# First bias of two head pairs read back in four pieces, small weights placed ahead of GpSimd's masks, first copies of reciprocals moved to VectorE

## The chip, the core and the metric

The kernel runs on one core of a Trainium2 chip. The metric is the device time of one execution in microseconds. The engines work side by side, each through its own queue in order: TensorE (PE, with its weight loads as PEld), VectorE (DVE), ScalarE (ACT), GpSimd (POOL) and SyncE (SP), which here issues most of the transfers.

## What is computed

An attention layer with a learned bias on relative positions, then a dense layer with a gated norm, then a layer of eight experts with two chosen for each token. Only the first touches the change:

```python
scores = scale * np.matmul(q, k.transpose(0, 1, 3, 2))        # 2 batches, 8 heads, 576 x 576, 64 wide
psi_rel = np.log1p(np.abs(rel)); psi_i = np.log1p(np.maximum(pos[:, None], 1.0))
x = (psi_rel / psi_i)[..., None]
h = np.maximum(x @ w1 + b1, 0.0)                               # 32 hidden units
bias = h @ w2                                                  # one value for query, key and head
scores = scores + bias.transpose(2, 0, 1)[None]
attn = np.exp(scores - scores.max(-1)); attn = attn / (attn.sum(-1) + 1e-9)
out = np.matmul(attn, v)
```

## The kernel before

A hidden unit is on or off depending on where |query - key| lies against a threshold, so the bias is made from masks. One **m** stands for 32 queries; there are 18. `masks(m, ...)` makes eight masks of 128 x 576 (four queries by 32 hidden units on the partitions), each on VectorE, ScalarE or GpSimd by the letters of MASK_ENG0 (m = 0: VectorE and ScalarE in turn), MASK_ENG1 (m = 1 to 6: GpSimd for masks 1 and 6, VectorE for 4, ScalarE for the other five) and MASK_ENG2 (from m = 7: five on GpSimd, three on VectorE). Masks have three buffers (`mk`). `mix(m, gg)`, called twice for an m, multiplies four masks with the small weights `WD` on TensorE (L204; slopes and intercepts, each as two fp16 parts), and VectorE joins them into the bias tile `t` (L209, L210; three buffers). After the second call SyncE writes `t` to a scratch tensor in DRAM, `biasd` (L212), since the bias is made with the queries in another order over the partitions than the scores need.

The small weights: `wab`, `W`, the scaling of `W`, and `WD` with its remainder are seven short operations on GpSimd (L150 to L173), with a power of two as scale that VectorE finds in between (L160 to L167).

Attention then goes over five blocks of 128 queries (`it`), four pairs of heads (`hp`) and two batches (`b`), one step k for each. `bias_in(n)` reads the bias of block it = n // 4 and pair hp = n % 4 back from `biasd` into the tile `bt` (128 x 2 x 576, six buffers); a block needs four m, so `bias_in(0)` and `bias_in(1)` need the writes of m = 0 to 3. `qk` makes scores (L308), adds bias and finds the row's extreme in one VectorE operation (L317), and ScalarE takes the exponential (L324). `tr` transposes the result, and, at the second batch, makes reciprocals of the sums (L343, L344) and spreads them over 64 columns into `rb` (L347, on GpSimd). `av` transposes `rb` (L359), multiplies with v (L368) and scales on VectorE (L372).

The program's order: all masks of m = 0, the products of m = 0 to 5 (twelve calls of `bias_step`, each of which also asks for masks of the next m), then `bias_in(0)` and `bias_in(1)`, then the steps k, each with one further `bias_step`, a `bias_in` at every second step, and from step 4 on the conversion of 64-bit weights, spread over the engines. The order on each engine's queue is not this one: the framework's scheduler simulates the program ahead of time, and whenever an engine is free it hands it the earliest instruction that is ready. `tc.keep_in_program_order(i)` pins an instruction behind the instruction that was written before it for the same engine. `tc.high_priority()` around the small weights puts them first among what is ready.

Of the kernel before, what the change touches and what calls it, by code (L numbers as in the profile page):

```python
# [9 lines left out]
F32 = mybir.dt.float32  # L10
# [6 lines left out]
OP = mybir.AluOpType  # L17
# [3 lines left out]
B, H, S, D = 2, 8, 576, 64  # L21
# [10 lines left out]
EB = 8  # L32
LAG = 2
PRE = 6
XB = 9
WB = 12
XS = (2, 2, 2, 2, 0, 1, 0, 1, 2)
# [27 lines left out]
def build(tc, I, O):  # L65
    nc = tc.nc
    ctx = ExitStack()
    with ctx:
        _build(tc, nc, ctx, I, O)


def _build(tc, nc, ctx, I, O):
# [4 lines left out]
    biasd = dram.tile([NG, 128, S], F32, name="biasd")  # L77
# [8 lines left out]
    V, P_ = nc.vector, nc.gpsimd  # L86
# [3 lines left out]
    def pool(stack, name, **kw):  # L90
        return stack.enter_context(tc.tile_pool(name=name, bufs=1, **{"reuse_waits": "tile", **kw}))

    xap, bp = pool(px, "xap"), pool(px, "bp")
    kvp, btp, ap = pool(pa, "kvp"), pool(pa, "btp"), pool(pa, "ap")
# [6 lines left out]
    def dbank():  # L101
        return psum.tile([128, 2, 512], F32, name="d", bufs=3)
# [27 lines left out]
    thr = bp.tile([128, 2, NQ], F32, name="thr")  # L130
# [45 lines left out]
    def engine(m, u):  # L176
        return (MASK_ENG0 if m == 0 else MASK_ENG1 if m < PRE + 1 else MASK_ENG2)[u]

    MK, TT = {}, {}

    def masks(m, lo, hi):

        if lo == 0:
            MK[m] = bp.tile([128, 8, S], BF, name="mk", bufs=3)
        for u in range(lo, hi):
            q, dst = 8 * m + u, MK[m][:, u]
            w = T[:, 572 - 4 * q:1148 - 4 * q]
            e = engine(m, u)
            if e == "A":
                nc.scalar.activation(dst, w, AF.Sigmoid, bias=thr[:, 1, q:q + 1], scale=STEP)  # L190
            else:
                (V if e == "D" else P_).tensor_scalar(dst, w, thr[:, 0, q:q + 1], None, op0=OP.is_gt)  # L192

    def mix(m, gg):

        if gg == 0:
            TT[m] = bp.tile([128, 2, S], F32, name="t", bufs=3)
        mk, G = MK[m], 2 * m + gg
        sl, ic = dbank(), dbank()
        for a, ps in enumerate((sl, ic)):  # L200
            for half in range(2):
                for n in range(2):
                    for u in range(4):
                        nc.tensor.matmul(ps[32 * u:32 * u + 32, half, 0:288], WD[n][:, 32 * a:32 * a + 32],  # L204
                                         mk[:, 4 * gg + u, half * 288:half * 288 + 288],
                                         start=(n == 0), stop=(n == 1))
        th = TT[m][:, gg].rearrange("p (a b) -> p a b", a=2)
        Lw = L[:, 560 - 16 * G:560 - 16 * G + S].rearrange("p (a b) -> p a b", a=2)
        V.scalar_tensor_tensor(th, Lw, inv[:, G:G + 1], sl[:, :, 0:288], op0=OP.mult, op1=OP.mult)  # L209
        V.scalar_tensor_tensor(th, ic[:, :, 0:288], unscale, th, op0=OP.mult, op1=OP.add)  # L210
        if gg == 1:
            nc.sync.dma_start(biasd[2 * m:2 * m + 2].rearrange("g p j -> p g j"), TT.pop(m))  # L212

    def bias_step(s):

        m, gg = divmod(s, 2)
        if m >= NM:
            return
        if m + 1 < NM:
            masks(m + 1, 4 * gg, 4 * gg + 4)  # L220
        mix(m, gg)

    BT = {}

    def bias_in(n):

        it, hp = divmod(n, 4)
        if it > 4:
            return
        r = 8 if it < 4 else 4  # L230
        src = biasd[8 * it:8 * it + r].rearrange("g (q h) j -> (g q) h j", h=H)[:, 2 * hp:2 * hp + 2]
        t = BT[it, hp] = btp.tile([128, 2, S], F32, name="bt", bufs=6)
        if it < 4:
            nc.sync.dma_start(t, src)
        else:
            for x in range(2):
                nc.sync.dma_start(t[64 * x:64 * x + 64, 0], src[:, x])
# [62 lines left out]
    def qk(it, hp, b):  # L300

        n, k = 2 * hp + b, KV[hp, b]
        if it < 4:
            ss = [dbank() for x in range(2)]
            for a in range(2):
                for x in range(2):
                    h = slice(64 * x, 64 * x + 64)
                    nc.tensor.matmul(ss[x][:, a, 0:288], Q[it][h, n], k[h, a * 288:a * 288 + 288], start=True, stop=True)  # L308
        else:
            ss = [dbank()]  # L310
            for a in range(2):
                nc.tensor.matmul(ss[0][:, a, 0:288], Q[it][:, n], k[:, a * 288:a * 288 + 288], start=True, stop=True)
        es = []
        for x, ps in enumerate(ss):
            e = ap.tile([128, S], F32, name="e", bufs=EB)
            nm = ap.tile([128, 1], F32, name="nm", bufs=6)
            V.tensor_tensor_reduce(out=e.rearrange("p (a b) -> p a b", a=2), in0=ps[:, :, 0:288],  # L317
                                   in1=BT[it, hp][:, x].rearrange("p (a b) -> p a b", a=2),
                                   scale=-0.125, scalar=3.0e38, op0=OP.add, op1=OP.min, accum_out=nm)
            es.append((e, nm))  # L320
        u = unit(it, hp)
        c = b * len(es)
        for x, (e, nm) in enumerate(es):
            nc.scalar.activation(e, e, AF.Exp, bias=nm, scale=-1.0, accum_out=u.sums[:, c + x:c + x + 1])  # L324
        ES[it, hp, b] = [e for e, nm in es]

    def tr(it, hp, b):

        u, es = SU[it, hp], ES.pop((it, hp, b))
        n = len(es)  # L330
        if b == 0:
            u.rest = psum.tile([128, 4, 128], F32, name="rest")
        pt = dbank().rearrange("p x (j i) -> p x j i", j=4)
        for x, e in enumerate(es):
            for jb in range(4):
                nc.tensor.transpose(pt[:, x, jb], e[:, jb * 128:jb * 128 + 128], ident)  # L336
        for x, e in enumerate(es):
            nc.tensor.transpose(u.rest[:, n * b + x], e[:, S - 128:S], ident)
        nc.scalar.activation(u.et[:, n * b:n * b + n, 0:4], pt[:, 0:n], AF.Copy)  # L339
        if b == 1:  # L340
            nc.scalar.activation(u.et[:, 0:2 * n, 4], u.rest[:, 0:2 * n], AF.Copy)
            u.rs = ap.tile([128, 4], F32, name="rs", bufs=3)
            V.tensor_scalar(u.rs[:, 0:2 * n], u.sums[:, 0:2 * n], 1e-9, None, op0=OP.add)  # L343
            V.reciprocal(u.rs[:, 0:2 * n], u.rs[:, 0:2 * n])  # L344
            if n == 2:
                u.rb = ap.tile([128, 4, 64], F32, name="rb", bufs=2)
                P_.tensor_copy(u.rb, u.rs[:, :, None].to_broadcast([128, 4, 64]))  # L347

    def av(it, hp):

# [21 lines left out]
        V.tensor_tensor(out=dst, in0=dst, in1=o[:, 1, :, 0:n], op=OP.mult)  # L372

    masks(0, 0, 8)
    for s in range(2 * PRE):
        bias_step(s)
    tc.keep_in_program_order(nc.scalar.preload_act_table_set("natural_log_exp_and_others"))
    bias_in(0)
    bias_in(1)
    chunks = list(range(16))  # L380
    raws, conv = [], []
    for k in range(len(A) + LAG + 8):
        if k % 2 == 0 and k < len(A):
            bias_in(k // 2 + 2)
        if k % 8 == 6 and k // 8 + 1 < 5:
            load_q(k // 8 + 1)
        if LAG <= k < len(A) + LAG:
            tr(*A[k - LAG])
        if LAG <= k - 1 < len(A) + LAG and A[k - 1 - LAG][2] == 1:
            av(*A[k - 1 - LAG][:2])  # L390
        if k < len(A):
            qk(*A[k])
        bias_step(2 * PRE + k)
        if k == CONV[0] - 3:
            raws = [words(chunks.pop(0)) for c in range(RB64)]
        if k in CONV:
            n = CONV.index(k)
            conv.append([5] + (conv_out(n, raws.pop(0)) if n < 8 else conv_in(*divmod(n - 8, 2), raws.pop(0))))
        for fs in conv:
            if len(fs) > 1:  # L400
                fs.pop(1)()
                fs[0] -= 1
                if fs[0] == 0 and chunks:
                    raws.append(words(chunks.pop(0)))
# [81 lines left out]
    def stage2(t, mid):  # L486
        lt = LT.pop(t)
        po = (abank, tbank)[t % 2 if AB else 0]()
        for f in range(8):
            for n, (wx, ww) in enumerate(PASSES):  # L490
                nc.tensor.matmul(po, lt[wx][:, f], WO[f][ww], start=(f == 0 and n == 0), stop=(f == 7 and n == 2))
            if f == FM:
                mid()
        x1 = X1[t] = mp.tile([128, 512], F32, name="x1", bufs=XB)
        nc.scalar.activation(x1, po, AF.Copy, scale=ST.pop(t)[:, 7:8])
# [304 lines left out]
    for e in range(E):  # L800
        W2 = [wload(w2s(e, f), ep, W2B, held=True) for f in range(4)] if e else []
        xt, w1 = XG.pop(e), W1.pop(e)
        for f in range(8):
            ph = psum.tile([128, 512], F32, name="phe", tag="h", bufs=3)
            for k in range(4):
                for n, (ww_, wx) in enumerate(PAS):
# [4 lines left out]
                                   op0=OP.max, op1=OP.subtract)  # L811
# [125 lines left out]
```

## Time and profile before

| | |
|---|---|
| time, median of 3 | 634.76 us (633.47 to 637.0) |
| the profiled execution's own time | 632.79 us |
| its span, first to last instruction | 630.9 us |
| TensorE busy | 581.1 us, 92% |
| VectorE busy | 392.2 us, 62% |
| ScalarE busy | 339.7 us, 54% |
| GpSimd busy | 229.3 us, 36% |
| mean granted clock of TensorE | 0.984 of 2.4 GHz |
| largest transfers: weights of the experts | 64 loads of 512 KB |
| writes of the bias | 18 of 576 KB |
| reads of the bias | 16 of 576 KB |

The shares are averages over stages with different limits: what a change to one stage is worth is read from that stage. All times inside the run are counted from the start of the span.

### The profile page before, as it was taken

The numbers are of one execution on the slowest core, as the hardware profiler recorded it, in microseconds if no ns is written. First come the engines' busy times: TensorE is split into PE (matmuls) and PEld (weight loads), VectorE is DVE, ScalarE is ACT, GpSimd is POOL, SyncE is SP. The second block draws the span as 40 slices with busy tenths as digits, with TensorE's granted clock in tenths as the row PEclk, the third lists the DMA queues.
The fourth block names the chain that finished last, engine by engine and source line by source line (L and its number), as shares of the span: only waits on it lengthen the run. The fifth ranks groups of instructions, "written<-read, shape, count | busy, mean of one in ns | idle before, by whom it ended". The sixth has DMA issues, their size and how long they took to land. (4 is left out here: it accounts for less than half of the span.)

```text
span 630.9 us, 12806 instructions
## 1 busy us (share of the span) xinstructions
PE 581.1 (92%) x5068; PEld 475.8 (75%) x5068; DVE 392.2 (62%) x913; ACT 339.7 (54%) x657; POOL 229.3 (36%) x173
## 2 busy tenths in 40 slices
PE   0879999999999999999999989999999999999990
PEld 0547766767677776888888788989898989898980
DVE  4978889998755636645347968674746464554400
ACT  6935756565678767534337436454545455544410
POOL 4999998990022148000003003221222222222111
PEclk9989999999999999999999989999999999999997
DMA  8675535627532135200405055756566565735212
GB/s 315 261 258 185 213 126 208 240 91 272 204 114 68 52 98 173 85 18 34 151 18 162 23 201 154 206 188 172 196 164 214 146 232 128 240 52 194 35 19 30
DMA packets 36247, 93.64 MB, mean 148 GB/s; under 512 B 3856, under 2 KB 5392, under 8 KB 36176
## 3 DMA queue, kind: packets, MB, share of 16 engines
q1 hardware_dynamic: 28784, 76.23, 33.7%
q0 software_dynamic: 5808, 13.37, 10.5%
q10 hardware_dynamic: 1584, 3.11, 1.4%
q8 instruction: 42, 0.69, 0.5%
q14 instruction: 29, 0.24, 0.1%
HBM read 69.76 MB, written 22.94 MB: 147 GB/s over the span
## 5 line engine op out<-in xcount | busy, mean ns | idle before, releaser
L192 POOL TENSOR_SCALAR mk<-T,thr 128x576 bf16<-128x576 f16 x67 | 119.7, 1805 | 10.7 <-PE d L204 7.2
L807 PE MATMUL phe<-xgt,wp 128*128 128x320 f32 x768 | 117.3, 312 | 2.3 <-ACT xgt L409 2.3
L807 PEld LDWEIGHTS phe<-xgt,wp 128*128 128x128 f32 x768 | 114.6, 190 | 3.0 <-ACT xgt L409 2.5
L641 POOL DMA_INDIRECT out<-y,si x24 | 39.0, 1623 | 149.6 <-ACT y L797 73.1
L790 PE MATMUL poe<-wp,hT 128*128 128x512 f32 x384 | 91.0, 393 | 0.0
L790 PEld LDWEIGHTS poe<-wp,hT 128*128 128x128 f32 x384 | 71.0, 188 | 14.2
L324 ACT ACTIVATE e<-e,nm 128x576 f32<-128x576 f32 x72 | 55.3, 770 | 43.6 <-DVE nm L317 43.6
L204 PE MATMUL d<-mk,wd 128*32 128x288 bf16 x1152 | 49.2, 298 | 26.5 <-POOL wd L171 14.4
L204 PEld LDWEIGHTS <-wd 128*32 128x32 f16 x1152 | 29.6, 98 | 47.7 <-issue 24.0
L810 DVE SCALAR_TENSOR_TENSOR hT<-phe,hT 128x320 fp32r<-128x320 f32 x64 | 31.3, 489 | 51.6 <-ACT hT L809 51.3
L317 DVE CUSTOM_DVE_ANT_0 e<-d,bt 128x576 f32<-128x576 f32 x72 | 51.9, 753 | 12.0 <-PE d L308 7.2
L410 DVE TENSOR_TENSOR wp<-w2raw,wp 128x1024 fp32r<-128x1024 f32 x32 | 39.1, 1225 | 19.2 <-ACT wp L409 17.4
L809 ACT ACTIVATE hT<-phe 128x320 fp32r<-128x320 f32 x64 | 28.0, 438 | 42.6 <-PE phe L807 42.6
L308 PE MATMUL d<-kv,q 64*128 64x288 f32 x256 | 48.0, 438 | 0.3 <-DVE t L210 0.3
L368 PE MATMUL av<-et,kv 128*64 128x128 f32 (+1 forms) x800 | 47.3, 266 | 0.0
L669 POOL DMA_INDIRECT xg<-x1d,gi x21 | 21.7, 1033 | 63.3 <-DVE si L631 47.3
L368 PEld LDWEIGHTS av<-et,kv 128*64 128x64 f32 x800 | 41.2, 137 | 4.4 <-issue 3.9
L336 PE MATMUL d<-ident,e 128*128 128x128 f32 x288 | 40.7, 283 | 2.1 <-ACT et L339 1.9
L339 ACT ACTIVATE et<-d 128x1024 f32<-128x1024 f32 (+1 forms) x40 | 37.2, 930 | 9.1 <-PE d L336 9.1
L452 PE MATMUL ps<-mk,xs 128*128 128x512 f32 x162 | 39.7, 397 | 2.1 <-DVE so L461 1.2
L336 PEld LDWEIGHTS d<-ident,e 128*128 128x128 f32 x288 | 31.9, 143 | 12.8 <-DVE nm L317 6.9
L409 ACT ACTIVATE wp<-w2raw 128x1024 fp32r<-128x1024 f32 x32 | 34.0, 1061 | 13.1 <-DMA w2raw<-moe_w 6.4
(193 smaller groups left out, 958.6 us busy)
## 6 DMA issues: line engine op xcount, KB each, us to landing
wraw<-moe_w SPq DMA_DIRECT2D x32, 512.0 KB, 7.5
w2raw<-moe_w SPq DMA_DIRECT2D x32, 512.0 KB, 6.1
biasd<-t SPq DMA_DIRECT2D x18, 576.0 KB, 3.7
bt<-biasd SPq DMA_DIRECT2D x16, 576.0 KB, 5.9
kv<-kv SPq DMA_DIRECT2D x8, 608.0 KB, 10.0
raw<-w_out SPq DMA_DIRECT2D x8, 512.0 KB, 4.7
raw<-w_in SPq DMA_DIRECT2D x8, 512.0 KB, 3.5
q<-q SPq DMA_DIRECT2D x5, 512.0 KB, 5.0
```

The lines of the kernel that those rows point to most:

```text
L192: (V if e == "D" else P_).tensor_scalar(dst, w, thr[:, 0, q:q + 1], None, op0=OP.is_gt)
L204: nc.tensor.matmul(ps[32 * u:32 * u + 32, half, 0:288], WD[n][:, 32 * a:32 * a + 32], mk[:, 4 * gg + u, half * 288:half * 288 + 288], star ...
L308: nc.tensor.matmul(ss[x][:, a, 0:288], Q[it][h, n], k[h, a * 288:a * 288 + 288], start=True, stop=True)
L317: V.tensor_tensor_reduce(out=e.rearrange("p (a b) -> p a b", a=2), in0=ps[:, :, 0:288], in1=BT[it, hp][:, x].rearrange("p (a b) -> p a b", ...
L324: nc.scalar.activation(e, e, AF.Exp, bias=nm, scale=-1.0, accum_out=u.sums[:, c + x:c + x + 1])
L336: nc.tensor.transpose(pt[:, x, jb], e[:, jb * 128:jb * 128 + 128], ident)
L368: nc.tensor.matmul(o[64 * x:64 * x + 64, 0, b, 0:n], v[:, jb, 64 * x:64 * x + 64], w, start=(jb == 0), stop=(jb == JB - 1))
L410: return a, V.tensor_tensor(out=lo, in0=src, in1=hi.bitcast(F32), op=OP.subtract)
L452: nc.tensor.matmul(ph[:, a], xs[wx][:, k], WI[k, a][ww], start=(k == 0 and n == 0), stop=(k == 3 and n == 2))
L641: nc.gpsimd.indirect_dma_start(out=dst, out_offset=bass.IndirectOffsetOnAxis(ap=si, axis=0), in_=y, in_offset=None, compute_op=OP.add, bou ...
L790: nc.tensor.matmul(po, hT[f][wh][:, j:j + R], W2[f // 2][ww_][:, c:c + N], start=(f == 0 and m == 0), stop=(f == 7 and m == 2))
L807: nc.tensor.matmul(ph[:, 0:CAP], w1[k][ww_][:, f * 128:f * 128 + 128], xt[wx][:, k], start=(k == 0 and n == 0), stop=(k == 3 and n == 2))
```

## The change

Three edits. First, `bias_in(0)` and `bias_in(1)` no longer read a whole tile after the twelve calls: behind each of the writes of m = 0 to 3, the 32 queries of that m are read into 32 partitions of each of the two tiles. Second, GpSimd's two masks of m = 1 are pinned behind what was written before them for GpSimd, which is the last of the small weights. Third, in the first block (it = 0) the copies into `rb` run on VectorE instead of GpSimd, four in all.

```diff
+EARLY = 2
@@ masks
-                (V if e == "D" else P_).tensor_scalar(dst, w, thr[:, 0, q:q + 1], None, op0=OP.is_gt)
+                i = (V if e == "D" else P_).tensor_scalar(dst, w, thr[:, 0, q:q + 1], None, op0=OP.is_gt)
+
+                if m == 1 and e == "P":
+                    tc.keep_in_program_order(i)
@@ mix
             nc.sync.dma_start(biasd[2 * m:2 * m + 2].rearrange("g p j -> p g j"), TT.pop(m))
+            if m < 4:
+                for n in range(EARLY):
+                    bias_in(n, m)
@@
-    def bias_in(n):
+    def bias_in(n, m=None):
+
 
         it, hp = divmod(n, 4)
         if it > 4:
+            return
+        if m is not None:
+            if m == 0:
+                BT[it, hp] = btp.tile([128, 2, S], F32, name="bt", bufs=6)
+            nc.sync.dma_start(BT[it, hp][32 * m:32 * m + 32],
+                              biasd[2 * m:2 * m + 2].rearrange("g (q h) j -> (g q) h j", h=H)[:, 2 * hp:2 * hp + 2])
             return
@@ tr
-                P_.tensor_copy(u.rb, u.rs[:, :, None].to_broadcast([128, 4, 64]))
+
+                (V if it == 0 else P_).tensor_copy(u.rb, u.rs[:, :, None].to_broadcast([128, 4, 64]))
@@
-    bias_in(0)
-    bias_in(1)
+    for n in range(EARLY, 2):
+        bias_in(n)
```

## Rows read from the trace of the kernel before

**Rows 1.** Busy time by stage: stretch, then PE, PEld, DVE, ACT, POOL, clock, DMA, GB/s.
```profile
14.40:37.40 23.00, 18.69 (x396) 11.69 (x398) 20.71 (x31) 19.07 (x28) 22.92 (x16) 1.00 0.67 241
37.40:48.10 10.70, 7.96 (x81) 5.43 (x81) 7.16 (x16) 3.25 (x8) 10.70 (x7) 0.68 0.77 301
...
69.30:79.90 10.60, 10.34 (x146) 7.83 (x144) 9.16 (x20) 6.62 (x13) 9.70 (x7) 1.00 0.32 109
79.90:91.10 11.20, 10.48 (x146) 7.82 (x144) 10.35 (x24) 6.62 (x13) 9.88 (x7) 1.00 0.28 102
```

**Rows 2.** Timeline of GpSimd: start, duration (us), instruction [idle before it, and its releaser].
```profile
9.50 1.92 POOL L192 TENSOR_SCALAR mk<-T,thr 128x576 bf16<-128x576 f16 x1 [3.41 <-DVE T L146]
11.40 0.56 POOL L154 TENSOR_TENSOR W<-wab,sp 128x32 f32<-128x32 f32 x2
11.94 1.79 POOL L192 TENSOR_SCALAR mk<-T,thr 128x576 bf16<-128x576 f16 x1
13.71 0.32 POOL L168 TENSOR_SCALAR W<-W,am 128x64 f32<-128x64 f32 x1
...
15.00 40.99 POOL L192 TENSOR_SCALAR mk<-T,thr 128x576 bf16<-128x576 f16 x24
```

**Rows 3.** Timelines of VectorE and, last, ScalarE, from the start to the first score.
```profile
8.48 0.15 DVE L165 RECIPROCAL am<-am 128x1 f32<-128x1 f32 x1
...
9.44 2.69 DVE L192 TENSOR_SCALAR mk<-T,thr 128x576 bf16<-128x576 f16 x6
16.05 0.81 DVE L209 SCALAR_TENSOR_TENSOR t<-L,sp,d 128x576 f32<-128x576 f32 x1 [3.91 <-PE d L204]
...
39.97 0.76 DVE L317 CUSTOM_DVE_ANT_0 e<-d,bt 128x576 f32<-128x576 f32 x1 [2.80 <-DMA bt<-biasd]
...
9.44 22.75 ACT L190 ACTIVATE mk<-T,thr 128x576 bf16<-128x576 f16 x34 [0.59 <-DVE T L146]
```

**Rows 4.** Timeline of SyncE's queue: each line is one or more transfers issued.
```profile
19.55 7.70 SPq L212 DMA_DIRECT2D biasd<-t  x3
27.30 1.20 SPq L120 DMA_DIRECT2D q<-q  x1
29.95 0.36 SPq L212 DMA_DIRECT2D biasd<-t  x1
30.36 0.46 SPq L693 DMA_DIRECT2D cst<-c_p  x1
34.49 0.33 SPq L234 DMA_DIRECT2D bt<-biasd  x1
34.92 0.39 SPq L212 DMA_DIRECT2D biasd<-t  x1
```

**Rows 5.** Transfers issued near 9.8, 23.4, 29.9 and 30.4 us; last, us to landing.
```profile
kv<-kv SPq DMA_DIRECT2D x2, 608.0 KB, 10.8
...
biasd<-t SPq DMA_DIRECT2D x1, 576.0 KB, 2.8
...
biasd<-t SPq DMA_DIRECT2D x1, 576.0 KB, 4.5
...
cst<-c_p SPq DMA_DIRECT2D x1, 2.0 KB, 4.3
```

**Rows 6.** TensorE's timeline; then groups of 41.3 to 48.1 and 48.1 to 58.7 us.
```profile
40.79 0.71 PE L204 MATMUL d<-mk,wd 128*32 128x288 bf16 x16 [2.73 <-DVE nm L317]
...
L308 PE MATMUL d<-kv,q 64*128 64x288 f32 x8 | 3.0, 724 | 0.0
...
L308 PE MATMUL d<-kv,q 64*128 64x288 f32 x16 | 2.9, 428 | 0.0
```

**Rows 7.** Single lines of the kernel: duration min/median/max (ns), first and last start, form.
```profile
L347 POOL COPY rb<-rs x10: 395/579/582, 55.9 to 146.5; 128x256 f32<-128x256 f32 x10
...
L372 DVE TENSOR_TENSOR XA<-XA,av x4: 422/422/423, 59.8 to 92.2; 128x256 f32<-128x256 f32 x4
...
L343 DVE TENSOR_SCALAR rs<-sums x10: 156/622/628, 47.4 to 146.0; 128x4 f32<-128x4 f32 x10
```

## The prediction

> **What bounds the kernel now.** I read the profile by stage first [rows 1], then followed, inside the early stages, each engine's own timeline back from the wait that ends last. From 48 us on TensorE is the fullest engine: in the pair of heads at 69.3 to 79.9 us it is busy for 10.34 of 10.60 us, in the next one for 10.48 of 11.20, with VectorE close behind at 10.35. It sets the pace from there, and whatever arrives earlier at 48 us arrives earlier at the end. None of the edits touches that work. Before it lie two stages that TensorE doesn't set. From 14.4 to 37.4 us, where the bias products of m = 0 to 5 are made (L204, L209, L210), VectorE is busy for 20.7 of 23.0 us, and TensorE waits for it. From 37.4 to 48.1 us nothing is full: TensorE has 8.0 busy us in 10.7 at a granted clock of 0.68.
>
> Two waits open these stages. The first product needs the small weights WD, and GpSimd makes them behind two masks: it sits idle from 6.1 to 9.5 us, takes a mask, makes W, takes another mask, and only then scales, rounds and splits W, done at 15.00 [rows 2]. VectorE, ready at 12.13, stands until 16.05 [rows 3]. The second: VectorE has finished its last product at 37.17 and stands 2.80 us until 39.97 for the first bias read back (L317 waits for bt). That read was issued at 34.49, after SyncE's queue had waited for the fourth write, issued at 29.95, to land [rows 4]. TensorE stands 2.73 us with it [rows 6].
>
> **The change, part by part.** All the times below are inside the profiled execution, 632.79 us with a span of 630.9. The median of three is 634.76, so 1.97 is added back at the end.
>
> *Weights ahead of the masks.* The pins hold the two GpSimd masks of m = 1 behind WD. Without them GpSimd makes W (0.56 us) in its idle time; scaling needs the reciprocal that VectorE ends at 8.63 [rows 3]; from there to WD complete it took 13.71 to 15.00, 1.29 us, so WD is complete at 9.92 instead of 15.00. Next late are the masks of m = 0: ScalarE's second is ready at 9.44 + 2 x 0.669 = 10.78 (34 masks in 22.75 us). From complete weights to the first L209 it took 1.05 us, so that one could start at 11.8; VectorE's six masks end at 12.13. So the chain starts at about 12.15, **3.9 us earlier**. Does something else become late inside it? VectorE needs (37.17 - 16.05)/6 = 3.52 us an m. ScalarE's five masks an m take 3.35 us and are not moved: the last of m = 5 is ready at 9.44 + 29 x 0.669 = 28.8, before the chain's new end at 33.3. GpSimd's two take 2 x 1.71 = 3.42 us an m from 9.92, those of m = 6 are ready at 30.4. Both keep ahead, by little. The bounds of this term are 0 (the weights don't move) and 3.9.
>
> *First bias in pieces.* One read of 576 KB becomes four of 144 KB, for two head pairs: two loads go, eight come. Each piece needs one write landed, and it stands in SyncE's queue, where a waiting read holds all that is behind it: the later writes, the loads of the next q, and at the end bt of the other two head pairs. The row for what that costs is the bt load of 34.49 itself: the queue stood from 30.8, and the fifth write, behind it, went out at 34.92. So what counts is the order that the scheduler gives the queue. The trace shows something of it [rows 4]. The next q load has a free buffer from the start (two buffers), and so has the load of cst; yet the first goes out behind the third write, the second behind the fourth. So up to the third write the schedule always had something more urgent for SyncE, and a read of the first piece, which can't be ready before the first write lands, should come behind the second write at least. I take that order. Then the fourth write's data is ready at 29.95 - 3.9 = 26.05; up to six pieces at about 0.4 us of issue stand ahead of it, I take 27.2. A write lands 2.8 to 4.5 us after its issue [rows 5], I take 3.6, since reads are in flight beside it: 30.8. No row shows a read of a piece. Nearest are the write that landed in 2.8 and the 2 KB load that took 4.3 behind others; a quarter of a load should be near the lower end, I take 3.0: 33.8. VectorE's chain ends at 33.27. So L317 starts at 33.9 instead of 39.97, **6.1 us earlier**, of which 3.9 come from the weights and 2.2 from the wait. Bounds: 6.7 (bt never late) and 2.8 (28.4 + 4.5 + 4.3 = 37.2).
>
> *Clock.* Behind the stand of TensorE the granted clock falls: over 37.4 to 48.1 it is 0.68, so 0.32 x 10.7 = 3.4 us of TensorE's time are lost, and the same matmuls of L308 take 724 ns there and 428 ns later [rows 1, 6]. If the stand is under 1 us, as in my forecast, TensorE goes from products to scores as busy as in 14.4 to 37.4, where the clock was whole. Part of the loss lies beside waits for VectorE and ScalarE, so I take half: **1.7 us**, bounds 0 and 3.4.
>
> *Copies of the reciprocals on VectorE.* Four copies of 128x256 leave GpSimd (0.40 to 0.58 us each) and come to VectorE. Nearest on VectorE is L372, the same size, 0.42 us; beside GpSimd's masks a tiny VectorE operation on the same numbers, L343, grows from 0.16 to 0.62 us, so 0.42 to 0.9 us each [rows 7]. Three fall into pairs of heads like that of 69.3 to 79.9, where VectorE has 1.4 us of slack (hidden); the fourth falls into 79.9 to 91.1, where it has 0.85 and TensorE 0.7 [rows 1]. I charge one: **0.4 us lost**, bounds 0 and 0.9. On GpSimd a copy stands behind masks of 1.7 us each; with TensorE 7 us earlier that would come nearer to being a wait, so this edit guards the gain rather than adding to it.
>
> A rule speaks against this edit. The Trainium skill, page "SBUF — State Buffer", section "SBUF: two separate sides", says that VectorE's two-port operations and GpSimd hold a shared pair of ports in turn, each for a whole instruction. By it a copy could wait for a whole mask, 1.71 us, and the charge would be, as an estimate, 2.1 instead of 0.4 us. The trace shows L343 held back by 0.47 us at the median, never by 1.7, so the sum goes by that.
>
> Sum: 6.1 + 1.7 - 0.4 = **7.4 us**; 632.79 becomes 625.4, and at the level of the median 634.76 becomes **627.4**. By its bounds (2.8 + 0 - 0.9 and 6.7 + 3.4 - 0) this case gives 624.7 to 632.9.
>
> **The rivals.**
> *Each read directly behind its write.* For: in the trace the first bt load stands ahead of the fifth write, though both could have gone the other way, so the schedule thinks a write lands sooner than it does. Then every m costs a full turn of the queue: about 0.4 of issue and 3.4 of landing, 3.8 us, slower than VectorE's 3.52. The first write, though 3.9 us earlier, queues behind the kv loads, whose last lands near 9.9 + 10.8 = 20.7; it lands near 22.5. Three turns make 33.9, the piece 3.0 to 3.3 more: L317 at 37.2. That is 2.8 us earlier, with TensorE's stand and the low clock kept: 2.4 us in all, **632.4**.
>
> *The weights don't move.* The pins hold m = 1 alone. VectorE ran a mask of m = 2 among its six before the first product, so masks of m = 2 can be ready early, and GpSimd may be handed those in the pinned ones' place. Against: between scaling, rounding and splitting W no mask was put in, though each waits for the one before. Then VectorE still ends at 37.17, the fourth write goes out near 31 and the piece is in at 37.6: 2.4 us, 1.7 of clock, less 0.4: **631.1**.
>
> *Slower.* The pieces look early to the schedule, so it puts the first L317 ahead of products in VectorE's queue, which runs in order. VectorE then stands until the piece is there (37.2 by the first rival), with n products of 1.76 us each behind it. The stage ends at 37.2 + 1.5 for the two L317 + 1.76 n, against 39.97 + 1.5 = 41.4 before: a loss from n = 2 on. With n = 4 it is 45.7, 4.3 slower, and 0.4 for the copies: **639.5**. Against: products come first in the program and VectorE had almost always one ready.
>
> **How the numbers follow.** The forecast has 0.52, reads behind writes 0.20, unmoved weights 0.17, slower 0.11. The predicted time is that of the forecast, 627.4. The range takes in its bounds and the two middle rivals, with 2 us for what the two sets of runs differ by: 624.7 to 634.4; the slower case stays out. About 0.5%, 3.2 us, is what a measurement here can tell from no change. Faster by more: 0.50 of the forecast, 0.05 of the first rival, 0.09 of the second, 0.64. Within it: 0.02, 0.15 and 0.08, 0.25. Slower: 0.11.
>
> **What would show it.** In the timeline of GpSimd WD complete near 9.9 with both masks behind it; the first L209 near 12.2; in SyncE's queue the second write ahead of the first piece, and the fourth write near 27; the first L317 near 34 with under 1 us of idle time before it; a granted clock of 1.0 from 34 to 45; the first four copies in VectorE's rows at 0.4 to 0.9 us; everything from the first conversion on 7 us earlier. I am wrong if SyncE waits for a write to land before each next one, if L317's wait stays near 3 us, or if L317 stands ahead of a product.

## The result, and the profile after

| | before | after |
|---|---|---|
| median of 6 runs each, side by side | 633.56 us (631.87 to 637.0) | 627.36 us (626.23 to 629.09) |
| ratio, 95% interval | | 0.9901 (0.9874 to 0.9929) |
| the profiled execution / its span | 632.79 / 630.9 us | 627.43 / 625.6 us |
| mean granted clock | 0.984 | 0.988 |

The forecast was 627.4. The number was met, the working only in part: the gain is 6.2 us by these medians and 5.4 by the two profiled executions, not 7.4, and the kernel before came out 1.2 us lower here than in the three runs that the forecast was added to. The experiments also move most of the gain from one edit to another.

Busy time by stage of the changed kernel (the columns of [rows 1]):

```profile
14.40:37.40 23.00, 16.43 (x358) 9.88 (x346) 21.27 (x36) 19.03 (x29) 23.00 (x14) 1.00 0.82 302
37.40:48.10 10.70, 10.58 (x132) 7.56 (x136) 9.68 (x24) 7.59 (x16) 10.70 (x7) 1.00 0.82 293
69.30:79.90 10.60, 9.93 (x142) 7.48 (x131) 10.50 (x24) 6.39 (x13) 10.60 (x7) 1.00 0.34 108
79.90:91.10 11.20, 10.61 (x158) 7.90 (x149) 10.22 (x25) 6.64 (x13) 11.20 (x7) 1.00 0.38 129
```

The second line is the stage that had 7.96 busy us of TensorE at a clock of 0.68 in [rows 1]: it is full now, at 1.0. GpSimd has no idle time in any of the four.

GpSimd's timeline after (answers to [rows 2]; start, duration, instruction, idle time before it):

```profile
8.68 0.70 POOL L169 TENSOR_SCALAR W<-W,am 128x64 f32<-128x64 f32 x1 [2.14 <-DVE unscale L168]
10.23 0.24 POOL L174 CAST wd<-rest 128x64 f16<-128x64 f32 x1
10.44 83.19 POOL L193 TENSOR_SCALAR mk<-T,thr 128x576 bf16<-128x576 f16 x47
93.59 0.81 POOL L362 COPY rb<-rs 128x256 f32<-128x256 f32 x1
```

WD is complete at 10.44 instead of 15.00. Behind it stand 47 masks without a gap, and only then the fifth copy of reciprocals, the first that stays on GpSimd.

VectorE's timeline after (answers to [rows 3]):

```profile
9.31 2.09 DVE L193 TENSOR_SCALAR mk<-T,thr 128x576 bf16<-128x576 f16 x5
11.96 0.81 DVE L213 SCALAR_TENSOR_TENSOR t<-L,sp,d 128x576 f32<-128x576 f32 x1 [0.56 <-PE d L208]
...
24.03 1.54 DVE L213 SCALAR_TENSOR_TENSOR t<-L,sp,d 128x576 f32<-128x576 f32 x2 [1.42 <-DMA biasd<-t]
...
34.30 1.58 DVE L193 TENSOR_SCALAR mk<-T,thr 128x576 bf16<-128x576 f16 x3
35.81 0.80 DVE L213 SCALAR_TENSOR_TENSOR t<-L,sp,d 128x576 f32<-128x576 f32 x1
36.53 0.74 DVE L331 CUSTOM_DVE_ANT_0 e<-d,bt 128x576 f32<-128x576 f32 x1
...
42.85 0.28 DVE L362 COPY rb<-rs 128x256 f32<-128x256 f32 x1
```

The first product starts at 11.96 (16.05 before), the first L331 (L317 before) at 36.53 (39.97 before), with three masks and a further product directly ahead of it and no idle time. At 24.03 there is a wait that the kernel before doesn't have: the next tile `t` isn't free, because an early write of the bias hasn't landed.

SyncE's queue after (answers to [rows 4]), and then transfers issued at 15.5, 23.9 and 31.6 us with their time to landing (as in [rows 5]):

```profile
15.53 3.77 SPq L216 DMA_DIRECT2D biasd<-t  x2
23.95 2.21 SPq L241 DMA_DIRECT2D bt<-biasd  x4
26.25 1.17 SPq L216 DMA_DIRECT2D biasd<-t  x2
30.24 2.83 SPq L241 DMA_DIRECT2D bt<-biasd  x4
33.17 1.61 SPq L216 DMA_DIRECT2D biasd<-t  x2
```

```profile
biasd<-t SPq DMA_DIRECT2D x1, 576.0 KB, 8.4
...
bt<-biasd SPq DMA_DIRECT2D x4, 144.0 KB, 2.6
...
bt<-biasd SPq DMA_DIRECT2D x1, 144.0 KB, 3.4
```

Two writes, four pieces, two writes, four pieces: the order of the forecast. The first write took 8.4 us to land. It was issued while the loads of k and v, issued up to 10.4 us, were still moving.

TensorE's timeline after, at the fifth copy:

```profile
92.69 0.38 PE L352 MATMUL rest<-ident,e 128*128 128x128 f32 x2
94.45 0.44 PE L374 MATMUL av<-ident,rb 128*128 128x128 f32 x2 [1.38 <-POOL rb L362]
```

It stands 1.38 us for that copy. The table says where the lead over the kernel before arose and went: the start of the same instruction in the profile before, less that in the profile after.

| kernel | first product | first conversion with bias | the same, step k = 2 | first use of `rb` (L359 before, L374 after) | median lead at 140 to 150 us | at 600 us |
|---|---|---|---|---|---|---|
| before: its times | 16.05 | 39.97 | 49.99 | 56.64 | | |
| after: lead | 4.1 | 3.4 | 6.9 | 6.9 | 5.3 | 5.3 |

4.1 us come from the weights, 0.7 of it is lost by the first conversion, 3.5 are won over the two steps behind that, and 1.6 are given back, with the wait at 94 us. From there the lead stays.

Part of the 3.5 is work moved. VectorE of the kernel before waits 2.80 us idle ahead of the first conversion and takes three masks just ahead of step k = 2:

```profile
48.30 1.77 DVE L192 TENSOR_SCALAR mk<-T,thr 128x576 bf16<-128x576 f16 x3
```

The changed kernel takes three masks and one product more ahead of the first conversion (34.30 to 36.53) and so has as many fewer between that and k = 2. The two conversions lie 6.5 us apart in it and 10.0 in the kernel before, or 8.6 in a second profile of the kernel before in which the clock stayed at 1.0 (e12_before_again below). So about 1.4 of the 3.5 goes with the clock and about 2.1 with that order; this split is an estimate from these three profiles.

### The profile page after: what moved, and what is told of

It reads as the page before. It is cut to its first block, busy times and chain, and to the rows that moved or that the text cites. A ratio compares the mean times of both kernels' runs of the same rounds, so it can differ in the third digit from the quotient of the medians.

```text
span 625.6 us, 12814 instructions
## 1 busy us (share of the span) xinstructions
PE 579.5 (93%) x5068; PEld 474.8 (76%) x5068; DVE 393.2 (63%) x917; ACT 339.7 (54%) x657; POOL 229.7 (37%) x169
## 5 line engine op out<-in xcount | busy, mean ns | idle before, releaser
L331 DVE CUSTOM_DVE_ANT_0 e<-d,bt 128x576 f32<-128x576 f32 x72 | 51.8, 752 | 8.2 <-PE d L322 6.2
```

## The experiments

The three edits can be had singly and in pairs, so the eight combinations say what each is worth. Ratios are against the kernel before run beside it (634.98, 634.11 and 634.10 us in the three sets of experiments, 633.56 for the changed kernel). They are not the quotients of the two medians, from which they differ by up to 0.002.

| weights ahead (pins) | reads in pieces | copies on VectorE | kernel | median us | ratio (95%) |
|---|---|---|---|---|---|
| | | | before | | 1 |
| x | | | e5_pins_only | 634.20 | 0.9991 (0.9967 to 1.0015) |
| | x | | e6_pieces_only | 635.58 | 1.0023 (1.0000 to 1.0047) |
| x | x | | e3_copies_gpsimd | 633.60 | 0.9988 (0.9960 to 1.0015) |
| | | x | e11_copies_only | 630.52 | 0.9927 (0.9903 to 0.9951) |
| x | | x | e2_whole_reads | 629.12 | 0.9912 (0.9880 to 0.9944) |
| | x | x | e1_no_pins | 628.98 | 0.9918 (0.9887 to 0.9949) |
| x | x | x | after | 627.36 | 0.9901 (0.9874 to 0.9929) |

Without the copies nothing is gained, whatever else is done. With them each of the other two edits adds 0.0009 to 0.0017, 0.6 to 1.1 us, which is inside the intervals.

The leads in the profiles of these and the other kernels, with the columns of the table above:

| kernel | first product | first conversion | k = 2 | first use of `rb`: time, lead | 140 to 150 us | 600 us |
|---|---|---|---|---|---|---|
| e12_before_again | -0.3 | 0.4 | 1.8 | 57.81, -1.2 | -1.2 | -1.3 |
| e5_pins_only | 3.8 | 4.7 | 5.6 | 55.71, 0.9 | -1.0 | -1.1 |
| e6_pieces_only | 0.1 | -1.1 | 0.7 | 57.23, -0.6 | -0.6 | -0.6 |
| e3_copies_gpsimd | 3.8 | 3.1 | 6.8 | 56.27, 0.4 | -1.5 | -1.6 |
| e11_copies_only | 0.1 | 0.5 | 0.5 | 56.10, 0.5 | 0.3 | 1.8 |
| e2_whole_reads | 3.8 | 5.4 | 5.7 | 50.99, 5.7 | 5.9 | 2.1 |
| e1_no_pins | 0.1 | 0.2 | 3.7 | 52.99, 3.7 | 4.4 | 4.2 |
| e4_five_copies | 3.8 | 3.2 | 6.7 | 49.91, 6.7 | 7.0 | 6.2 |
| e10_eight_copies | 3.6 | 3.1 | 6.6 | 50.09, 6.6 | 6.0 | 3.1 |
| e8_late_kv | 3.9 | 1.4 | 3.9 | 52.70, 3.9 | 3.7 | 5.0 |
| e9_late_kv_eight_copies | 4.0 | 3.5 | 6.3 | 50.34, 6.3 | 5.5 | 5.4 |
| e7_copies_and_filler | 0.0 | 0.2 | -2.1 | 58.77, -2.1 | -2.4 | -1.3 |

### One edit taken out of the three

Copies back on GpSimd:

```diff
-                (V if it == 0 else P_).tensor_copy(u.rb, u.rs[:, :, None].to_broadcast([128, 4, 64]))
+                P_.tensor_copy(u.rb, u.rs[:, :, None].to_broadcast([128, 4, 64]))
```

> The changed kernel with the first four copies of the reciprocals back on GpSimd. Theory: GpSimd's queue is full from 10.4 us on, so four copies of 0.4 us in it move its end of the stretch 1.6 us later, TensorE waits for copies in the first block already, and the end comes 1.6 us later: about 629.0. Rival, the copies are hidden on either engine: 627.4. Rival, VectorE pays more for them than GpSimd did: 626.5 to 627.

Measured: 633.6, 4.6 us more than expected. TensorE's and GpSimd's timelines and one stretch by busy time:

```profile
49.66 0.38 PE L352 MATMUL rest<-ident,e 128*128 128x128 f32 x2
56.27 0.69 PE L374 MATMUL av<-ident,rb 128*128 128x128 f32 x2 [6.23 <-POOL rb L362]
```

```profile
10.78 45.09 POOL L193 TENSOR_SCALAR mk<-T,thr 128x576 bf16<-128x576 f16 x26
55.83 0.39 POOL L362 COPY rb<-rs 128x256 f32<-128x256 f32 x1
```

```profile
53.00:60.10 7.10, 3.83 (x32) 3.50 (x34) 0.00 (x0) 0.00 (x0) 7.10 (x6) 0.52 0.76 263
```

The reciprocals were ready in time, but their copy stands behind 26 masks in GpSimd's queue, which has been full since 10.78. TensorE stands 6.23 us, its granted clock is half over most of 53 to 60 us, and a lead of 6.8 us becomes a loss of 1.5.

The pins taken out:

```diff
-                if m == 1 and e == "P":
-                    tc.keep_in_program_order(i)
```

> The changed kernel without the pins on GpSimd's two masks of m = 1. Theory: the weights stand behind two masks again, so the first L209-type product starts near 16.0 us instead of 12.0 and VectorE's products of m = 0 to 5 end near 37.2 instead of 34.4; but GpSimd's queue, which in the changed kernel runs from 10.4 to 93.6 us without a gap and holds TensorE for 1.4 us at the first copy left to it, ends that stretch only about 1.1 us later. So the end comes 1.1 us later than the changed kernel's: about 628.5. Rival, the pins are worth what they move the first product: 3 to 4 us later, 630.5 to 631.4. Rival, the pins are worth nothing because the first write of the bias stands behind the kv loads either way: 627.4.

Measured: 628.98, near the theory's 628.5; the interval of the ratio takes in 630.5 of the rival too, so the time doesn't decide. In the profiles the lead at 140 to 150 us is 1.0 us below that of the changed kernel, where the theory had 1.1. The products start at 15.94 and the first conversion comes at 39.82, no earlier than before, yet at step k = 2 the lead is 3.7: the granted clock was 1.0 all through, where [rows 1] has 0.68, and VectorE again took three masks and a product ahead of the first conversion.

The pieces taken out:

```diff
-EARLY = 2
+EARLY = 0
```

> The changed kernel with the first two bias tiles read whole, as before; pins and VectorE copies kept. Theory: the products start near 12.0 us, but the first L317-type addition has to wait for a whole read issued after the fourth write has landed, at about 37 us, with 2 to 3 us of idle time on VectorE and the granted clock at half behind it: about 3 us faster than the kernel before, 630.5, and 3 us slower than the changed one. Rival, the pieces gain nothing since SyncE's queue waits for every write anyway: 627.4.

Measured: 629.12 against 630.5 expected, which the interval takes in. VectorE's timeline at the first conversion, and the landing of the two whole reads, issued at 30.33 and 31.86:

```profile
34.61 0.76 DVE L331 CUSTOM_DVE_ANT_0 e<-d,bt 128x576 f32<-128x576 f32 x1 [0.60 <-DMA bt<-biasd]
```

```profile
bt<-biasd SPq DMA_DIRECT2D x1, 576.0 KB, 4.1
...
bt<-biasd SPq DMA_DIRECT2D x1, 576.0 KB, 6.8
```

With whole reads the first conversion comes 1.9 us earlier than with pieces, after a wait of 0.60 us and not of 2 to 3. The first tile is complete at 34.5; in the changed kernel its last piece, issued at 31.59 behind those of m = 2, took 3.4 us, so that it is complete at 35.0. The pieces bring the first tile no earlier here. The second they do bring earlier, at 35.4 instead of 38.6, and at its first use, k = 2, the changed kernel is 1.3 us ahead of this one, though no wait for that tile shows in either. What this kernel loses against the changed one in the end, it loses at 160 us, where its lead falls from 5.9 to 2.3; ScalarE's timeline and then TensorE's:

```profile
158.11 0.67 ACT L261 ACTIVATE t<-raw 128x512 f32<-128x512 f32 x1 [2.38 <-DMA w32d<-t]
```

```profile
159.74 2.05 PE L208 MATMUL d<-mk,wd 128*32 128x288 bf16 x32 [2.06 <-ACT et L353]
```

A conversion of weights waits for its tile, whose last write to DRAM is under way, ScalarE's exponentials queue behind it, TensorE stands 2.06 us and the half clock follows (from 159.9 for 3.4 us). The changed kernel doesn't have this wait; e1_no_pins, e5_pins_only and e10_eight_copies have it too. What makes it come was not tried.

### One edit alone

Each is the kernel before with one edit of the diff above.

> The kernel before with the two pins of m = 1 alone; whole reads behind the twelve calls, all copies of reciprocals on GpSimd. My theory (taken from the run with the copies put back, where TensorE stood 6.2 us for the first copy behind 26 masks): the lead of 3.9 us is there at the first product and at the first score, and is lost where the first copy stands behind GpSimd's masks, so 633 to 635 us against 634 to 635 of before, a ratio of 0.997 to 1.002, and TensorE stands 3 to 7 us for the copy before the first transposition of the reciprocals. Rival: the copy is only late when pins and pieces come together, and the pins alone bring 3 to 4 us: 630.5 to 631.5.

Measured: 634.2, as the theory had it. TensorE's timeline:

```profile
50.79 0.38 PE L352 MATMUL rest<-ident,e 128*128 128x128 f32 x2
55.71 0.69 PE L374 MATMUL av<-ident,rb 128*128 128x128 f32 x2 [4.54 <-POOL rb L362]
```

The lead was 5.6 us at k = 2; a stand of 4.54 us and the clock behind it took all of it.

> The kernel before with the reads of the first two pairs in pieces alone; no pins, all copies on GpSimd. The products start at 16 us as before. My theory: the first conversion with bias comes about where it came in the run without pins (40 us), the clock stays whole there as in that run, and TensorE then waits for the first copy behind GpSimd's masks, so that under 1 us is left: 633.5 to 635.5 us, a ratio of 0.997 to 1.002. Rival: the whole clock alone, 3.7 us of lead in the run without pins, stays to the end: 630.5 to 631.5.

Measured: 635.58, a little above the theory's 635.5. The way there was another: the first conversion came at 41.03, the granted clock was half from 36.6 us for 10.2 us, and TensorE still stood 1.10 us for the copy. TensorE's timeline:

```profile
57.23 0.44 PE L372 MATMUL av<-ident,rb 128*128 128x128 f32 x2 [1.10 <-POOL rb L360]
```

> The kernel before with the four copies of the first block on VectorE alone. In the kernel before the first copy ends at 56.35 us and TensorE needs it at 56.64, so nothing waits for it. My theory: no change, 634 to 635.5 us, a ratio of 0.998 to 1.002. Rival: GpSimd's masks and casts behind the copies come 2.3 us earlier, which carries to the end: 632 to 633.

Measured: 630.52, 3.6 us below the kernel before by the medians (4.6 by the ratio). My theory of no change fell, and the rival's 632 to 633 was too high as well. TensorE's timeline, and the stretch behind its stand:

```profile
40.30 1.15 PE L204 MATMUL d<-mk,wd 128*32 128x288 bf16 x16 [2.33 <-DVE nm L317]
...
56.10 0.38 PE L359 MATMUL av<-ident,rb 128*128 128x128 f32 x2
```

```profile
39.60:46.40 6.80, 6.09 (x58) 3.81 (x58) 6.06 (x13) 3.25 (x8) 6.80 (x5) 0.50 0.92 363
```

In this profile little differs from before until 360 us. So the kernel before was profiled a second time.

> The kernel before, unchanged, a second profile. The copies alone brought 3.6 us in the median, of which the two traces show 0.3 at 130 us and 1.5 from a half clock at 369 us that only the kernel before had. My theory: the copies lift a cap. With them on GpSimd the first transposition of reciprocals can't start before 55.7 to 57.2 us, as in the four traces that have them there, and what makes TensorE later than that adds to it, while with the copies on VectorE an early execution stays early. So the first transposition is again at 56.3 or later. Rival: it comes at 55 us or earlier, and there is no cap; then the 3.6 us come from elsewhere.

TensorE's and GpSimd's timelines of the kernel before in its second profile, and the stretch that had the half clock in the first:

```profile
40.37 0.67 PE L204 MATMUL d<-mk,wd 128*32 128x288 bf16 x16 [2.02 <-DVE nm L317]
...
54.59 0.38 PE L338 MATMUL rest<-ident,e 128*128 128x128 f32 x2
57.81 0.44 PE L359 MATMUL av<-ident,rb 128*128 128x128 f32 x2 [2.84 <-POOL rb L347]
```

```profile
19.31 38.10 POOL L192 TENSOR_SCALAR mk<-T,thr 128x576 bf16<-128x576 f16 x22 [0.62 <-ACT mk L190]
57.36 0.39 POOL L347 COPY rb<-rs 128x256 f32<-128x256 f32 x1
```

```profile
41.30:48.10 6.80, 6.63 (x74) 4.29 (x74) 6.80 (x16) 3.33 (x7) 6.80 (x5) 1.00 0.82 332
```

This is the cap that the expectation speaks of. The time was 634.09 us. Here the first conversion came 0.4 us earlier, TensorE stood 2.02 us instead of 2.73, its clock stayed at 1.0, and by k = 2 it was 1.8 us ahead of the first profile. Then it stood 2.84 us for the first copy and came out 1.2 us behind. The kernel before thus paid for its half clock in one profile and for the copy in the other. In the first the copy ended at 56.34 and was used at 56.64: a margin of 0.30 us that looked like no wait at all. In all five profiles with the copies on GpSimd the first use is at 55.71 to 57.81, whether TensorE was ready at 50 us or at 56; in the others it follows TensorE.

Set against this second profile, e11_copies_only is 3.6 us shorter in span (632.2 and 628.6): 1.7 of it at the first use, and most of the rest near 370 us, where the kernel before, in both its profiles, ran some us at half clock and e11 did not. Whether that second part belongs to the copies stays open (see the last section). The granted clock of every execution is on record and bounds the clock's whole share: a span times one less its granted clock, which is about the most that the half clock can have cost, is 8.2 us on average over the eight executions of e11_copies_only and 9.9 over the 31 of the kernel before, while the mean spans differ by 3.9 us. By this estimate at most some 1.7 of the 3.9 is clock, and over 2 us is not.

### The fifth copy, and the late write

One further copy on VectorE, or all eight of the first two blocks, in the changed kernel:

```diff
@@ five
-                (V if it == 0 else P_).tensor_copy(u.rb, u.rs[:, :, None].to_broadcast([128, 4, 64]))
+                (V if it == 0 or (it, hp) == (1, 0) else P_).tensor_copy(u.rb, u.rs[:, :, None].to_broadcast([128, 4, 64]))
@@ eight
-                (V if it == 0 else P_).tensor_copy(u.rb, u.rs[:, :, None].to_broadcast([128, 4, 64]))
+                (V if it <= 1 else P_).tensor_copy(u.rb, u.rs[:, :, None].to_broadcast([128, 4, 64]))
```

> The changed kernel with one more copy, the first of the second block, on VectorE. Theory: TensorE's wait of 1.4 us for that copy, behind 47 masks in GpSimd's queue, goes, and with it the loss of 1.7 us between 88 and 107 us; the next copy on GpSimd is ready some 3 us before it is needed, so nothing takes its place: about 625.8. Rival, VectorE is the bound there (its busy time before was 10.35 of 11.2 us a pair of heads) and the loss stays: 627.4.

> The changed kernel with the copies of the first two blocks (eight) on VectorE. In the kernel with five, the sixth and seventh copy ended 0.62 and 0.78 us ahead of their use, so nothing waited for them. My theory: as with five copies, 625 to 626.5 us, a ratio of 0.985 to 0.989, and no wait of TensorE for a copy. Rival: VectorE pays for each further copy, and the time is 1 us or more above that with five.

Measured: five 625.62, as expected, ratio 0.9874 (0.9835 to 0.9914); eight 627.0, above the expected 625 to 626.5, ratio 0.9882 (0.9843 to 0.9921). Of five, TensorE's timeline and GpSimd's:

```profile
93.43 0.38 PE L374 MATMUL av<-ident,rb 128*128 128x128 f32 x2
```

```profile
10.69 92.95 POOL L193 TENSOR_SCALAR mk<-T,thr 128x576 bf16<-128x576 f16 x52
```

The wait is gone, and the lead of 6.7 is still there at 150 us. GpSimd's unbroken row grows to 52 masks. Eight copies keep 6.0 and then meet the wait at 160 us. Both ratios lie below that of the changed kernel, and their intervals overlap with its own, so neither is shown to be faster.

The loads of k and v of the third and fourth pair, moved behind the twelve calls, where `True` pins them behind what was written before them for SyncE:

```diff
-    for hp in range(4):
+    def load_kv(hp, late=False):
...
+            if late:
+                tc.keep_in_program_order(i)
...
+    load_kv(0)
+    load_kv(1)
@@ behind the loop over bias_step(s)
+    load_kv(2, True)
+    load_kv(3, True)
```

> The changed kernel, with the loads of k and v of the third and fourth pair of heads issued behind the twelve calls, so that the first write of the bias doesn't stand in the queue behind them. My theory: the first write lands 3 to 5 us after its issue instead of 8.4, the product's wait of 1.42 us for a bias tile is gone, the first conversion with bias starts near 35 us instead of 36.5; at the end nothing of it is left, since the fifth copy of reciprocals is the 48th instruction of GpSimd's queue and ends at 94 us whatever TensorE does: 626.5 to 628 us at the level of 634 for the kernel before, a ratio of 0.988 to 0.992, with a wait of 2 to 3 us for the fifth copy. Rivals: the lead stays and the time falls to 625 to 626; or the late loads come too late for the third pair and the time rises to 629 and more.

Measured: 628.18, ratio 0.9910 (0.9878 to 0.9942), which is the ratio expected, but not for the reason expected. The first write's landing, VectorE's timeline and TensorE's:

```profile
biasd<-t SPq DMA_DIRECT2D x1, 576.0 KB, 3.7
```

```profile
37.84 0.82 DVE L219 SCALAR_TENSOR_TENSOR t<-d,unscale,t 128x576 f32<-128x576 f32 x1 [1.25 <-PE d L213]
```

```profile
36.64 1.15 PE L213 MATMUL d<-mk,wd 128*32 128x288 bf16 x16 [1.97 <-DVE t L218]
```

The write lands in 3.7 us, and the wait for a tile `t` is gone, so the loads did cause it. The time isn't won. VectorE now takes four masks and both products of the next m ahead of the first conversion, TensorE stands 1.97 us between those, the half clock follows from 36.5 us on, and the first conversion comes at 38.57, later than with the wait. The fifth copy was no limit, since TensorE came too late for it.

> The late loads, and the copies of reciprocals of the first two blocks (eight) on VectorE. My theory: the cap of the fifth copy is gone, so what the late loads bring is kept: about 1 us better than the eight copies alone, 623.5 to 625.5 us, a ratio of 0.983 to 0.987. Rival: the pace from 50 us on is VectorE's as much as TensorE's, and the four further copies cost as much as they bring: the same as the changed kernel.

Measured: 627.11, ratio 0.9906 (0.9875 to 0.9937), a miss: the first conversion came at 36.48, as in the changed kernel, and nothing was gained over it. Up to 50 us VectorE, ScalarE and GpSimd run the same instructions in the same order as in e8_late_kv, whose first conversion came at 38.57. So that order alone doesn't make it late: here TensorE stood 1.41 us and the half clock lasted 3.4 us from 37.3 on, there 1.97 us and 6.8 us.

### The clock by itself

The copies alone, and filler for TensorE's stand:

```diff
+        if k == 0:
+            idle = psum.tile([128, 512], F32, name="av")
+            for z in range(15):
+                tc.keep_in_program_order(nc.tensor.matmul(idle[:, 0:288], ident, T.bitcast(F32)[:, 0:288], start=True, stop=True))
```

> The kernel with the copies alone, and beside it 15 extra fp32 matmuls of 128 x 288 on TensorE behind the scores of the first step, into a bank that nothing reads, so that TensorE is busy where it stands 2.73 us in the kernel before; all else is computed as before. This tests the clock by itself. My theory: the granted clock is 1.0 over 41 to 48 us instead of half, the stages behind it come 1.5 to 3.5 us earlier, and the time is 1.5 to 3 us below the kernel with the copies alone. Rival: the half clock there lies beside waits for VectorE, and the extra matmuls bring nothing or delay the next scores: 0 to 1 us above the kernel with the copies alone.

Measured: 633.61, 3.1 us above the copies alone, outside both what the theory and what the rival had. TensorE's timeline:

```profile
37.51 7.54 PE L396 MATMUL av<-T,ident 128*128 128x288 f32 x30
```

I had sized the filler wrongly: 15 matmuls became 30 passes and 7.54 us, far more than the stand. The clock did stay at 1.0; what the passes cost, and what that gave back, can't be told apart in this time. Two pairs of profiles do it better. The second profile of the kernel before has the clock at 1.0, and its lead grew from 0.4 to 1.8 us over the stretch that ran at half clock in the first. And e6_pieces_only and e1_no_pins run the same instructions in the same order on VectorE, ScalarE and GpSimd up to VectorE's first copy of reciprocals, at 46.14 in the second. Their first products start 0.02 us apart, and in both TensorE stands 1.06 us near 35 us. Then the one ran at half clock for 10.2 us and the other not (busy time, clock in the third column from the right):

```profile
36.60:46.80 10.20, 9.28 (x81) 5.14 (x79) 7.62 (x16) 3.05 (x7) 10.20 (x7) 0.50 0.53 180
```

```profile
36.60:46.80 10.20, 9.01 (x114) 5.95 (x113) 10.20 (x24) 4.28 (x9) 10.20 (x6) 1.00 0.68 237
```

At k = 2 they are 3.0 us apart (49.30 and 46.34). That is what the clock cost in these two executions.

## The prediction against the runs

*Weights ahead of the masks.* Forecast: WD complete at 9.92, the first product at 12.15. Measured: 10.44 and 11.96. Right in time and in mechanism. What it is worth at the end was wrong: the lead of 4.1 us at the first product (3.9 forecast) is worth nothing alone (e5_pins_only) and about 1 us beside the copies, which is inside the intervals.

*Pieces.* The order in SyncE's queue was right, and so was the fourth write, near 27. Two sizes failed. The write took 4.5 us to land, not 3.6, and the first tile's last piece 3.4, not 3.0, so the tile was complete at 35.0 us and not at 33.8; and VectorE had begun on three masks and a product of the next m at 34.30, so that the first conversion came at 36.53 instead of 33.9. The term of 6.1 us was 3.4, but about 2.1 of what it lacks came back by k = 2 as work already done. The third part of the error was a wait of 1.42 us that the forecast didn't have: I had seen, in the first rival, that the first write queues behind the loads of k and v, but not asked who waits for the tile that it holds. None of the rivals came: the weights moved, no read stood directly behind each write, and VectorE did not stand for a read.

*Clock.* VectorE's wait was gone and the granted clock 1.0, as forecast; TensorE's longest stand there was 1.11 us, a little over the 1 us forecast. From the first conversion to k = 2 the lead grew by 3.5 us, which looks like the upper bound of the term (3.4). About 1.4 of it is clock by the second profile of the kernel before, near the 1.7 taken, and the rest is the work that VectorE had done ahead. But that second profile shows the kernel before with a whole clock there and no gain at the end. So the term can't be added to the kernel before as it stands.

*Copies.* This is the step that failed. I charged 0.4 us for them and called them a guard. The price was about right: 0.28 us for three of the four, 0.74 for the other. The worth was not: by the ratios, taking them out loses 5.5 us of the 6.3 (0.9988 less 0.9901), adding them alone brings 4.6 (0.0073; 3.6 by the medians), and nothing else brings anything without them. Every row for it was in [rows 2]: the 24 masks from 15.00 on take 40.99 us and end at 56, and [rows 7] has the first copy at 55.9. TensorE used it at 56.64. Whatever I forecast for the start, the first use could not come before the copy, and I had the number for that bound without comparing it with the forecast arrival, about 7 us earlier. I also didn't ask the same of the fifth copy, which the edit leaves behind 47 masks. It took 1.6 us back.

The Trainium skill's rule of the shared pair of ports (page "SBUF — State Buffer", section "SBUF: two separate sides"), by which a copy could wait for a whole mask, is not borne out for this operation: beside masks of 1.7 us no copy on VectorE took more than 0.74 us in the profiles of the kernels with five and eight copies, and none had idle time before it. Whether this copy is one of the two-port operations no run here shows.

*The sum.* 6.1 + 1.7 - 0.4 was forecast; the profile has 3.4 + 3.5, 6.9 at k = 2, less the 1.6 of the fifth copy, 5.3 us of span. That the time came out at 627.4 all the same is luck. The forecast for the profiled execution was 625.4 and it took 627.43; the 1.97 us added back, because the profiled execution of the kernel before lay that much under its median of three, covers this miss of 2.0, while that of the changed kernel lay at its median.

## To carry to other kernels

An engine that runs in order and is full is a clock of its own: add up what stands ahead of each short instruction that another engine waits for, and put that time beside the earlier arrival that is hoped for. An operation with 0.3 us to spare shows no wait and can still hold the whole gain back, so before a stage is made earlier, the margin of each operand behind it wants reading, not only its waits. Here the two edits that make a stage earlier earned nothing without the one that takes the short instruction off the full engine, and that one alone earned most of the gain, which only the combinations show.

## What the runs showed of the hardware

*The half clock isn't settled by the stand alone.* Behind a stand of 2.73 us the kernel before ran at half clock (1.2 of 2.4 GHz) from 41.3 us for 6.8 us; in its second profile, behind 2.02 us, it did not, and not behind its stand of 2.84 us for the copy either, as the clock in this stretch of that profile shows:

```profile
57.80:68.00 10.20, 9.93 (x138) 7.43 (x139) 5.62 (x13) 5.32 (x11) 10.20 (x7) 1.00 0.66 235
```

e11_copies_only did behind 2.33 us, and e6_pieces_only behind 1.06 us, where e1_no_pins didn't. In each of the 14 profiles TensorE has one stand of 2.26 or 2.27 us that ends between 363 and 372 us. In 8 of them 3.4 us of half clock begin within 1.2 us of its end, in 6 none. The same stretch in the kernel before and in e11_copies_only, by busy time, the clock in the third column from the right:

```profile
369.00:372.40 3.40, 3.12 (x12) 3.15 (x13) 0.93 (x3) 0.21 (x1) 0.00 (x0) 0.50 1.04 402
```

```profile
369.00:372.40 3.40, 3.32 (x23) 3.35 (x24) 1.22 (x3) 0.74 (x4) 0.00 (x0) 1.00 1.03 405
```

The lead of e11_copies_only grows there by 1.4 us. The Trainium skill, page "TensorE: Matmul & The Clock Gate", section "Part 1: The HAM clock gate (the "warmup" mystery)", says that the gate's window runs free of the kernel, so that the same kernel meets it at different points; the profiles agree as far as they go: like stands are followed by the half clock in one execution and not in another.

*A write queues behind the loads.* The first write of 576 KB took 8.4 us to land behind the loads of k and v, the last of which landed at 22.5, and 3.7 with half of them moved away; behind the first the second took 6.4, the third and fourth 4.0 and 4.5.
